# One planner, re-measured: attention with a parallel feed-forward on one core, with its sums normalised in place and zero matmuls in PE's free slots

## The chip, the core and the metric

The kernel runs on one core of a Trainium2 chip. The metric is the device time of one execution in microseconds (us). Its engines are PE (TensorE, matrix products into PSUM), ACT (ScalarE, activations), DVE (VectorE, elementwise work), POOL (GpSimd, here only setup) and SP, which issues the transfers.

## The reference

One normalised input feeds two branches, whose results are added to it. Attention has 32 query heads of width 20 and one shared key and value head, over 2048 positions.

```python
xn = _layernorm(x, axis=-1)                       # x: 1 x 2048 x 640
q = (xn @ wq).reshape(B, S, H, Dh).transpose(0, 2, 1, 3)   # H = 32, Dh = 20
k = xn @ wk                                       # one key head
v = xn @ wv
scores = jnp.einsum("bhqd,bkd->bhqk", q, k) * (Dh ** -0.5)
p = _softmax(scores, axis=-1)
o = jnp.einsum("bhqk,bkd->bhqd", p, v)
A = o.transpose(0, 2, 1, 3).reshape(B, S, H * Dh) @ wo
B_ = _silu(xn @ w1) @ w2                          # F = 1728
return x + A + B_
```

## The kernel before, in words

**Work.** The 2048 queries are cut into 4 chunks of 512. A unit is one head of one chunk; 128 units make 43 groups of 3 (the last has 2). A group walks over 16 tiles of 128 keys, one step each, 688 steps in all. A step t does the following.

- S (`do_S`, L616): up to three matmuls of 32 rows, one for each unit, write three 128x512 score banks; even and odd steps use two sets of three banks (`par3`). S of step t therefore waits until the readers of step t-2 are done.
- exp: ACT takes two or three banks in one instruction (L632) and writes them into a ring of `NBLK` slots, `E`. In a DVE step the third bank goes to DVE (L646), which computes the exponential from bits: after up to `ZB` = 4 such blocks, `flush_z` issues three instructions over all of them (L693, L696, L697). `want_dve` (L587) makes a step a DVE step when DVE's planned backlog is under `DVE_TH`.
- PV: the values times each block, four 32-column matmuls side by side (L656 for ACT's blocks, L662 and L664 for DVE's two factors), accumulated over the 16 steps in bank 6 (`UBANK`). A PV frees the slots of the ring that it read.

**End of a group** (`end_group`, L706). DVE copies bank 6 to `U` (L713). Then bank 6 is free for the next group. Four matmuls by a 0/1 matrix transpose `U` (L718) into bank 7 (`XBANK`), as a job among the others; DVE takes the reciprocal of the sums (L726) and multiplies (L743) into `o`.

**Projections.** All other matmuls are jobs that share bank 7, one after the other: queries of the next chunk (`q_job`, L755, evacuated by DVE at L767), the hidden layer (`h_job`, L781, tanh on ACT at L789 and product on DVE at L794), transposes of `o` (`oT_job`, L805) and the output (`out_job`, L828 and L834, evacuated at L841 or L848). `fill_chunk` (L872) gives each job the step from which it may start, evenly by number of jobs over `PACE` = 0.9 of the chunk's steps.

**Order.** Everything is unrolled by a planner (`Sched`) that runs before the kernel: each engine takes, at its planned time, the ready operation with the lowest priority number; durations are formulas such as `t_dve_ps`, and `LAT` is the delay until another engine sees a result. What comes out is a fixed order for each engine, with semaphore waits for each dependence on another engine. PE's order is made in `step` (L491). S comes first as soon as it is ready; otherwise PV or a job is chosen, in the mode that PE is in if possible, since another tile shape costs `SWITCH`; the choice is not made if it would end later than `limit`, which is when S is ready, or `S_LEAD` before the running exp ends, whichever is later. PV goes ahead of jobs when `PV_PRESS` = 6 steps are waiting.

**Prologue and tail.** The first 56 us load and normalise the input (statistics on DVE), transpose it and make keys and values, with the first steps among them. After the last step there remain the last output projections.

Of the kernel before, what the change touches and what calls it, by code (L numbers as in the profile page):

```python
# [15 lines left out]
P = 128  # L16
D = 640
H = 32
# [25 lines left out]
NBLK = 26  # L44
# [3 lines left out]
SWITCH = 0.10  # L48
S_LEAD = 0.62
PV_PRESS = 6  # L50
DVE_TH = 3.2
PACE = 0.9


class Op:
    __slots__ = ("eng", "dur", "fn", "deps", "prio", "seq", "end", "avail", "idx", "inc", "inc_no", "sem",
                 "on_sched", "name", "dma", "mode", "start", "mm")
# [207 lines left out]
def t_dve_ps(n):  # L265
    return n / 960.0 + 0.085
# [14 lines left out]
def t_act(n):  # L281
    return n / 1200.0 + 0.094
# [21 lines left out]
class Builder:  # L304
# [17 lines left out]
    def alloc(self):  # L322
# [36 lines left out]
        self.eps = sb([P, 1], F32)  # L359
        self.XS = 11  # L360
# [27 lines left out]
    def steps_init(self):  # L388
        self.groups = []
        u = 0  # L390
        while u < NUNITS:
            self.groups.append(list(range(u, min(u + 3, NUNITS))))
            u += 3
        self.NG = len(self.groups)
        self.T = self.NG * KT
        self.s_next = 0
        self.pv_q = deque()
        self.pv_wait = deque()
        self.misc = deque()
# [11 lines left out]
        self.pv_started = False  # L411
        self.pro_left = True
# [78 lines left out]
    def step(self, now):  # L491
# [51 lines left out]
        nxt = min(sr, pv_r, job_r)  # L543
        if choice is None:
            return nxt
        if choice == "PV":
            d = 0.216 + self.switch("PV")
        else:
            d = (job if job is not None else cand[0]).mms[0][0] + self.switch("M")
        if sr < INF and now + d > limit + 1e-9:  # L550
            return nxt if nxt > now else sr
        if choice == "PV":
            op = self.pv_q.popleft()
            op.dur = d
            if not self.pv_started:
                self.pv_started = True
                op.deps |= sc.deps_of((), [("B", UBANK)])
            self.pe_mode = "PV"
            sc.commit(op, now)
        else:  # L560
            if job is None:
                job = cand.popleft()
                job.bank = self.bank_for_job()[1]
                self.cur_job = job
            self.do_mm(job, now, d)
        return True
# [9 lines left out]
    def do_mm(self, job, now, d):  # L576
        fn = job.mms.pop(0)[1]
        b = job.bank
        op = self.sc.new("pe", d, lambda pe: fn(pe, b), job.reads, [("B", b)], name=job.name, queue=False)
        self.pe_mode = "M"  # L580
# [6 lines left out]
    def want_dve(self, t):  # L587
        if self.pro_left:
# [8 lines left out]
    def do_S(self, t, now):  # L597
# [12 lines left out]
        def fn(pe):  # L610
            ins = None
            for j, x in enumerate(us):
# [8 lines left out]
                    name=f"S{t}", queue=False)  # L621
        self.pe_mode = "S"
# [29 lines left out]
        def pfn(pe):  # L652
# [6 lines left out]
            if dv:  # L659
# [8 lines left out]
                    name=f"PV{t}", mode="PV", queue=False)  # L668
        self.pv_wait.append((pv, dv))
# [36 lines left out]
    def end_group(self, g):  # L706
        sc = self.sc
        us = self.groups[g]
        up = g % 2
# [4 lines left out]
        sc.new("dve", t_dve_ps(QW), evac, [("UB",)], [("U", up)], prio=2.0, name=f"Uev{g}")  # L714
        mms = []
        for qt in range(4):
            def f(pe, b, qt=qt):
                return pe.matmul(self.bk(b, qt * 64, qt * 64 + 64), self.U[0:rows, up, qt * P:(qt + 1) * P],  # L718
                                 self.stk[0:rows, :], start=True, stop=True)
            mms.append((0.16, f))  # L720

        def consume(b):
            xv = self.bk(b, 0, 256).rearrange("p (q z) -> p q z", q=4)[:, :, 0:63].rearrange(
                "p q (i r) -> p q i r", i=3)
            rl = self.rL[:, up, :, :]
            sc.new("dve", 0.11, lambda v: v.reciprocal(rl, xv[:, :, :, DH]), [("B", b)], [("rL", up)], prio=2.5,  # L726
                   name=f"rcp{g}")
            nh = len(us)
            for c in sorted(set(x // H for x in us)):
                js = [j for j, x in enumerate(us) if x // H == c]  # L730
                qs = [j if j < nh - 1 else 2 for j in js]
                h0 = us[js[0]] % H
                n = len(js)
                runs = [(qs, h0)]
                if qs != list(range(qs[0], qs[0] + n)):
                    runs = [([q], h0 + i) for i, q in enumerate(qs)]
                for rq, hh in runs:
                    m = len(rq)
                    dst = self.o[:, c % 2, :, hh * DH:(hh + m) * DH].rearrange("p q (i d) -> p q i d", d=DH)
                    src = xv[:, :, rq[0]:rq[0] + m, 0:DH]  # L740
                    r0 = rl[:, :, rq[0]:rq[0] + m]
                    rb = bass.AP(self.rL, r0.offset, [list(r0.ap[0]), list(r0.ap[1]), [1, m], [0, DH]])
                    sc.new("dve", t_dve_ps(4 * m * DH), lambda v, dst=dst, src=src, rb=rb: v.tensor_tensor(  # L743
                        dst, src, rb, ALU.mult), [("B", b), ("rL", up)],
                        [("o", c % 2, hh + i) for i in range(m)], prio=2.5, name=f"nrm{g}")
                self.norm_made[c] += n
        self.urgent.append(Job(f"UT{g}", mms, [("U", up), ("stk",)], consume))


    def q_job(self, c, ht, step=-1, act=False):  # L750
# [8 lines left out]
        def consume(b):  # L759
# [6 lines left out]
            else:  # L766
                sc.new("dve", t_dve_ps(QW), lambda v: v.tensor_scalar(dst, self.bk(b), C1, self.offq[:, :],  # L767
                                                                      ALU.mult, ALU.add),
                       [("B", b), ("offq",)], ks, prio=3.0, name=f"qev{c}_{ht}")
# [5 lines left out]
    def h_job(self, c, fk, step):  # L775
# [9 lines left out]
        def consume(b):  # L785
# [4 lines left out]
                   prio=3.0, name=f"th{c}_{fk}")  # L790
            ks = [("hT", fk)]
            if c == 0:
# [3 lines left out]
                [("B", b), ("tb", tp)], ks, prio=3.0, name=f"hp{c}_{fk}")  # L796
# [3 lines left out]
    def oT_job(self, c, i, step=-1):  # L800
        sc = self.sc
        mms = []
        for k in range(DC):
# [3 lines left out]
            mms.append((0.07, f))  # L807

        def consume(b):
            src = self.bk16(b)[:, 0:DC * P].rearrange("p (c t) -> p c t", c=DC)  # L810
            sc.new("dve", t_dve_ps(D), lambda v: v.tensor_copy(self.oT[:, :, i * P:(i + 1) * P], src),
                   [("B", b)], [("oT", i)], prio=3.0, name=f"oT{c}_{i}")
# [3 lines left out]
    def out_job(self, c, i, e, step=-1, ffn=True, attn=True):  # L816
# [21 lines left out]
        def consume(b):  # L838
            src = self.bk(b, 0, 320)
            if not attn:  # L840
                sc.new("dve", t_dve_ps(320), lambda v: v.scalar_tensor_tensor(  # L841
                    out=self.yx[:, i, e0:e0 + 320], in0=src, scalar=0.5, in1=self.xres[:, i, e0:e0 + 320],
                    op0=ALU.mult, op1=ALU.add), [("B", b), ("xres", i)], [("yx", i, e), ("w1",)], prio=3.0, name=f"y{n}_{e}")
# [6 lines left out]
                op0=ALU.mult, op1=ALU.add), [("B", b), rk], [("ost", sl, e)], prio=3.0, name=f"out{n}_{e}")  # L850
# [21 lines left out]
    def fill_chunk(self, c, t):  # L872
        jobs = []
        if c >= 1:
            for i in range(4):
                if c == 1:
                    self.load_xres(0, i)
                jobs.append(lambda s, i=i: self.oT_job(c - 1, i, s))
            for i in range(4):
                for e in range(2):  # L880
                    jobs.append(lambda s, i=i, e=e: self.out_job(c - 1, i, e, s))
        if c + 1 < QC:
            for ht in range(HT):
                jobs.append(lambda s, ht=ht: self.q_job(c + 1, ht, s))
        for fk in range(FC):
            jobs.append(lambda s, fk=fk: self.h_job(c, fk, s))
        if c == QC - 1:
            for i in range(4):
                for e in range(2):
                    jobs.append(lambda s, i=i, e=e: self.out_job(c, i, e, s, attn=False))  # L890
# [15 lines left out]
    def prologue(self):  # L906
# [52 lines left out]
        pool(0.2, lambda g: g.tensor_copy(self.idb[:, :], self.idf[:, :]), [("idf",)], [("idb",)])  # L959
        pool(0.1, lambda g: g.memset(self.eps[:, :], EPS), [], [("eps",)])  # L960
# [112 lines left out]
        def tr_job(n):  # L1073
            xs = n % 4
            mms = []
            for k in range(DC):
# [3 lines left out]
                mms.append((0.07, f))  # L1080

            def consume(b):
# [5 lines left out]
                else:  # L1088
                    sc.new("dve", t_dve_ps(D), lambda v: v.tensor_copy(dst, src), [("B", b)], [("xnT", n)],
# [115 lines left out]
```

## Time and profile before

| | |
|---|---|
| median of 3 runs | 910.75 us (904.34 to 915.66) |
| profiled execution | 904.07 us |
| its span, first to last instruction | 902.2 us |
| mean granted clock of PE | 0.888 |
| instructions | 15485, of them 6099 matmuls, 1281 on DVE, 755 on ACT |
| HBM | 11.36 MB read, 2.62 MB written, 15 GB/s over the span |

In the shares of busy time, each engine has its busy us, share of the span and number of instructions. PE's matmuls are pipelined and their ends are modelled, so that a matmul of 512 columns shows about 0.39 us although the next one starts 0.22 us after it. A group row has the line, the engine, the operation, what it writes and reads, its shape and count, then busy us, the mean ns of one, and the idle time of the engine just before, with what ended it. A row of the waits says who waited for whom: us in total, times, longest. In a table of windows each row has the stretch in us from the span's start, its length, busy us and count for each engine (PE, PEld for weight loads, DVE, ACT, POOL), the granted clock (1.00 is full), and the share and rate of DMA. In the timeline a row has its start, its length and what ran; "[0.35 <-DVE ...]" is the engine's idle time before it and what ended it.

### The profile page before, as it was taken

To read this page: it belongs to the slowest core of one execution; us is meant where nothing else is said; L and a number is where in the kernel's file an instruction comes from. 1 tells how busy PE (TensorE), PEld (TensorE's weight loads), DVE (VectorE), ACT (ScalarE), POOL (GpSimd) and SP (SyncE) were. 2 spreads that over 40 slices of the span, in tenths; PEclk is the share of its full clock that TensorE was granted. 3 is DMA by queue.
4 is the path that set the end of the run, shared out by engine and by line. 5 is a ranking of instruction groups with operands and counts; after the bars stand their busy time and mean duration, and the time that the engine had idled before them with its cause. 6 is when DMAs were issued, how large, how long until landed. Compare 5 with 4: busy or idle time off the path is not lost. (4 is left out here: it accounts for less than half of the span.)

```text
span 902.2 us, 15485 instructions
## 1 busy us (share of the span) xinstructions
PE 763.0 (85%) x6099; PEld 259.3 (29%) x6099; DVE 782.5 (87%) x1281; ACT 760.4 (84%) x755; POOL 26.5 (3%) x53
## 2 busy tenths in 40 slices
PE   4779887878889999888779999987789998888887
PEld 2322322222223432222213433222223342222334
DVE  7759989988888989899997999999978978878995
ACT  4469999998888799999988888999987868989980
POOL 4600000000000000000000000000000000000000
PEclk9589989887659999899967999999979898969999
DMA  9300000000000010000000000000000010000000
GB/s 305 113 1 1 1 1 2 1 1 1 1 1 16 16 30 1 1 1 1 1 1 1 30 16 16 1 1 1 1 1 1 30 31 1 1 1 1 1 1 30
DMA packets 12408, 14.97 MB, mean 17 GB/s; under 512 B 2544, under 2 KB 11696, under 8 KB 12336
## 3 DMA queue, kind: packets, MB, share of 16 engines
q1 hardware_dynamic: 11024, 13.93, 4.7%
q8 instruction: 49, 0.80, 0.4%
q10 hardware_dynamic: 1312, 0.05, 0.1%
q14 instruction: 23, 0.19, 0.1%
HBM read 11.36 MB, written 2.62 MB: 15 GB/s over the span
## 5 line engine op out<-in xcount | busy, mean ns | idle before, releaser
L632 ACT ACTIVATE sbt<-psall 128x1024 bf16<-128x1024 f32 (+2 forms) x688 | 730.6, 1143 | 104.8 <-PE psall L616 52.3
L646 DVE TENSOR_SCALAR sbt<-psall 128x512 int16<-128x512 f32 x503 | 340.7, 685 | 75.1 <-PE psall L616 72.4
L616 PE MATMUL psall<-sbt 32*128 32x512 bf16 x2048 | 293.2, 422 | 77.0 <-ACT sbt L632 57.6
L656 PE MATMUL psall<-sbt 128*32 128x512 bf16 x1545 | 226.1, 428 | 23.5 <-DVE sbt L697 12.1
L662 PE MATMUL psall<-sbt 128*32 128x512 bf16 x503 | 181.0, 426 | 0.0
L664 PE MATMUL psall<-sbt 128*32 128x512 bf16 x503 | 173.6, 428 | 0.0
L616 PEld LDWEIGHTS psall<-sbt 32*128 32x128 bf16 x2048 | 69.4, 92 | 319.3 <-ACT sbt L632 144.4
L696 DVE TENSOR_TENSOR sbt<-sbt 128x2048 bf16<-128x2048 bf16 x126 | 152.7, 1212 | 1.3
L781 PE MATMUL psall<-sbt 128*128 128x512 bf16 (+1 forms) x280 | 90.5, 422 | 7.6 <-DVE sbt L794 4.8
L656 PEld LDWEIGHTS psall<-sbt 128*32 128x32 bf16 x1545 | 55.0, 99 | 127.4 <-issue 54.1
L693 DVE TENSOR_SCALAR sbt<-sbt 128x2048 int16<-128x2048 int16 x126 | 86.7, 688 | 2.9
L828 PE MATMUL psall<-sbt 128*128 128x320 bf16 x448 | 85.1, 307 | 0.8 <-DVE sbt L841 0.4
L697 DVE TENSOR_SCALAR sbt<-sbt 128x2048 int16<-128x2048 int16 x126 | 85.5, 679 | 0.2
L828 PEld LDWEIGHTS psall<-sbt 128*128 128x128 bf16 x448 | 36.6, 98 | 43.6 <-issue 28.6
L755 PE MATMUL psall<-sbt 128*128 128x512 bf16 x160 | 45.1, 390 | 3.0 <-DVE sbt L767 1.7
L662 PEld LDWEIGHTS psall<-sbt 128*32 128x32 bf16 x503 | 41.5, 98 | 0.0
L794 DVE SCALAR_TENSOR_TENSOR sbt<-sbt,psall 128x512 bf16<-128x512 bf16 (+1 forms) x56 | 38.0, 678 | 2.5 <-ACT sbt L789 2.4
L718 PE MATMUL psall<-sbt 128*128 128x64 f32 x172 | 35.9, 311 | 4.5 <-DVE sbt L794 2.3
L789 ACT ACTIVATE sbt<-psall 128x512 bf16<-128x512 f32 (+1 forms) x56 | 34.3, 612 | 6.3 <-PE psall L781 4.5
L664 PEld LDWEIGHTS psall<-sbt 128*32 128x32 bf16 x503 | 37.4, 97 | 0.0
L781 PEld LDWEIGHTS psall<-sbt 128*128 128x128 bf16 (+1 forms) x280 | 21.1, 102 | 51.4 <-issue 26.7
L718 PEld LDWEIGHTS psall<-sbt 128*128 128x128 f32 x172 | 27.9, 214 | 25.0 <-issue 11.2
(67 smaller groups left out, 293.5 us busy)
## 6 DMA issues: line engine op xcount, KB each, us to landing
sbt<-in_A_x_dram SPq DMA_DIRECT2D x32, 160.0 KB, 2.9
out_dram<-sbt SPq DMA_DIRECT2D x16, 160.0 KB, 1.8
sbt<-in_B_w_dram SPq DMA_DIRECT2D x5, 432.0 KB, 6.7
sbt<-in_B_w_dram SPq DMA_DIRECT2D x13, 160.0 KB, 5.3
sbt<-in_A_wq_dram SPq DMA_DIRECT2D x5, 160.0 KB, 3.4
sbt<-in_A_wo_dram SPq DMA_DIRECT2D x5, 160.0 KB, 6.5
sbt<-in_B_w_dram SPq DMA_DIRECT2D x1, 80.0 KB, 5.7
sbt<-in_A_wk_dram ACTq DMA_DIRECT2D x1, 25.0 KB, 2.8
```

The source lines that it names most:

```text
L616: ins = pe.matmul(self.bk(par3 + j), self.kT[r:r + SLOT, kk, kt * P:(kt + 1) * P], self.qT[r:r + SLOT, h // 4, (x // H) % 2, :], start=Tru ...
L632: return a.activation(self.E[:, b0 * QW:(b0 + na) * QW], self.ps[:, par3 * BANK:(par3 + na) * BANK], AF.Exp, scale=ACT_SCALE)
L646: return v.tensor_scalar(self.Z[:, zs, zp * QW:(zp + 1) * QW], self.bk(bb), 0.0, ZMAX, ALU.max, ALU.min)
L656: ins = pe.matmul(self.bk(UBANK, 0, QW, q * SLOT, (q + 1) * SLOT), self.v[:, kt, :], self.E[:, (b0 + j) * QW:(b0 + j + 1) * QW], start=fir ...
L662: pe.matmul(self.bk(UBANK, 0, QW, 64, 96), self.v[:, kt, :], y, start=first, stop=last, tile_position=(0, 64))
L664: ins = pe.matmul(self.bk(UBANK, 0, QW, 96, 128), self.v[:, kt, :], z, start=(gd == 0), stop=(self.last_dve_kt[g] == kt), tile_position=(0 ...
L693: sc.new("dve", t_dve_4x(w), lambda v: v.tensor_scalar(Y, Z, 0x7F, 0x3F80, ALU.bitwise_and, ALU.bitwise_or), zk, yk, prio=4.0, name="u")
L696: sc.new("dve", t_dve_2x(w), lambda v: v.tensor_tensor(yb, zb, yb, ALU.mult), zk + yk, yk, prio=4.0, name="T1")
L697: sc.new("dve", t_dve_4x(w), lambda v: v.tensor_scalar(Z, Z, 0x7F80, None, ALU.bitwise_and), zk, zk, prio=4.0, name="B")
L718: return pe.matmul(self.bk(b, qt * 64, qt * 64 + 64), self.U[0:rows, up, qt * P:(qt + 1) * P], self.stk[0:rows, :], start=True, stop=True)
L781: return pe.matmul(self.bk(b, 0, QW, 0, rows), self.w1[:, k, fk * P:fk * P + rows], self.xnT[:, k, c * QW:(c + 1) * QW], start=(k == 0), s ...
L828: return pe.matmul(self.bk(b, 0, 320), self.hT[0:rows, fk, i * P:(i + 1) * P], self.w2[0:rows, fk, e0:e0 + 320], start=(m == 0), stop=(m = ...
```

## The change

All of it is in the planner and in how the order is made; the computation is the same.

1. The planner's durations and delays get other values (`LAT`, `t_dve_ps`, `t_act`, single entries), and its limits too (`S_LEAD`, `DVE_TH`, `SWITCH`). A last step of a group is never a DVE step (`NOD`).
2. U is transposed into bank 6 itself, as one operation of four matmuls in PV's own queue. The reciprocal and the product read bank 6, so the next group's PV waits for them. These operations and all evacuations get priorities under 1.0, ahead of DVE's first exponential step.
3. The ring has 34 slots instead of 26, and PV goes first when more than 25 of them are in use.
4. `fill`: where PE has nothing to do until S or the next work is planned, and its planned busy share over the last 3.4 us is under 0.72, it gets a matmul by a zeroed tile of up to 512 columns. While a group's sum is open, it adds zeros to bank 6; otherwise it writes bank 7 when that is free.
5. A job's starting step is spread by its cost instead of by number.

```diff
-NBLK = 26
+NBLK = 34
-SWITCH = 0.10
-S_LEAD = 0.62
-PV_PRESS = 6
-DVE_TH = 3.2
-PACE = 0.9
+SWITCH = 0.105
+S_LEAD = 0.56
+PV_PRESS = 9
+DVE_TH = 4.0
+U_PRIO = 0.9
+X_PRIO = 0.95
+PACE = (0.9, 0.9, 0.9, 0.9)
+WIN = 3.4
+FILL_BELOW = 0.72
+OVER = 0.1
+NOD = 1
-LAT = {"pe": 0.20, "act": 0.09, "dve": 0.06, "pool": 0.10, "sp": 0.0}
+LAT = {"pe": 0.215, "act": 0.175, "dve": 0.14, "pool": 0.15, "sp": 0.0}
 def t_dve_ps(n):
-    return n / 960.0 + 0.085
+    return n / 960.0 + 0.067
 def t_act(n):
-    return n / 1200.0 + 0.094
+    return n / 1200.0 + 0.051
...
-        press = len(self.pv_q) + len(self.pv_wait) >= PV_PRESS
+        used = sum(o.na for o in self.pv_q) + sum(o.na for o, _ in self.pv_wait)
+        press = used > NBLK - PV_PRESS
         choice = None
-        if pv_n and self.pe_mode == "PV":
+        if pv_n and (self.pe_mode == "PV" or press or self.pv_q[0].mode == "M"):
             choice = "PV"
-        elif has_misc and self.pe_mode == "M" and not (press and pv_n >= 2):
+        elif has_misc and self.pe_mode == "M":
             choice = "M"
...
         if choice is None:
-            return nxt
+            return self.fill(now, min(nxt, limit)) or nxt
...
-        if sr < INF and now + d > limit + 1e-9:
-            return nxt if nxt > now else sr
+        if sr < INF and now + d > limit + OVER:
+            return self.fill(now, limit) or (nxt if nxt > now else sr)
...
+    def fill(self, now, until):
+        if self.s_next >= self.T and not self.pv_q:
+            return None
+        sc = self.sc
+        mode = "PV" if self.u_open else "M"
+        room = min(until, now + 0.33) - now - self.switch(mode)
+        if room < 0.08 or self.busy_share(now) > FILL_BELOW:
+            return None
+        n = min(512, int(room * 2400) // 32 * 32)
+        if self.u_open:
+            ukey = None
+
+            def fn(pe):
+                return pe.matmul(self.bk(UBANK, 0, n, 0, 32), self.zero[:, 0:32], self.zero[:, 0:n], start=False,
+                                 stop=False, tile_position=(0, 0), skip_group_check=True)
+        else:
+            r, b = self.bank_for_job()
+            if self.cur_job is not None or r > now + 1e-9:
+                return None
+            ukey = ("B", b)
+
+            def fn(pe):
+                return pe.matmul(self.bk(b, 0, n), self.zero[:, 0:P], self.zero[:, 0:n], start=True, stop=True)
...
     def want_dve(self, t):
-        if self.pro_left:
+        if self.pro_left or t % KT >= KT - NOD:
             return False
...
-        sc.new("dve", t_dve_ps(QW), evac, [("UB",)], [("U", up)], prio=2.0, name=f"Uev{g}")
-        mms = []
-        for qt in range(4):
-            def f(pe, b, qt=qt):
-                return pe.matmul(self.bk(b, qt * 64, qt * 64 + 64), self.U[0:rows, up, qt * P:(qt + 1) * P],
-                                 self.stk[0:rows, :], start=True, stop=True)
-            mms.append((0.16, f))
+        sc.new("dve", t_dve_ps(QW), evac, [("UB",)], [("U", up)], prio=U_PRIO, name=f"Uev{g}")
+
+        def ut(pe):
+            ins = None
+            for qt in range(4):
+                ins = pe.matmul(self.bk(UBANK, qt * 64, qt * 64 + 64), self.U[0:rows, up, qt * P:(qt + 1) * P],
+                                self.stk[0:rows, :], start=True, stop=True)
+            return ins
+        op = sc.new("pe", 0.5, ut, [("U", up), ("stk",)], [("UB",)], name=f"UT{g}", mode="M", queue=False)
+        self.pv_wait.append((op, False))
...
-        span = PACE * (s1 - s0)
-        for k, mk in enumerate(jobs):
-            j = mk(s0 + int(span * k / len(jobs)))
-            self.misc.append(j)
+        span = PACE[c] * (s1 - s0)
+        tot = sum(w for w, _ in jobs)
+        at = 0.0
+        for w, mk in jobs:
+            self.misc.append(mk(s0 + int(span * at / tot)))
+            at += w
```

The weights w are 1.4 for a transpose of `o`, 3.6 for an output job (2.9 without attention), 2.2 for a query job and 3.0 for a hidden-layer job.

More of the change, by code (lines that the diff above doesn't have):

```diff
@@ L359, in alloc @@
         self.eps = sb([P, 1], F32)
+        self.zero = sb([P, 512], BF16)
         self.XS = 11
@@ L554, in step @@
             op.dur = d
+            op.work = 0.216
+            self.u_open = op.kt < KT - 1
+            self.pe_mode = op.mode
             if not self.pv_started:
@@ L565, in step, with busy_share @@
             self.do_mm(job, now, d)
+        return True
+    def busy_share(self, now):
+        a = now - WIN
+        tot = 0.0
+        for op in reversed(self.sc.order["pe"]):
+            if op.end <= a:
+                break
+            tot += op.end - max(a, op.end - op.work)
+        return tot / WIN
+    def fill(self, now, until):
[19 more added lines that the diff above has]
+                return pe.matmul(self.bk(b, 0, n), self.zero[:, 0:P], self.zero[:, 0:n], start=True, stop=True)
+        z = sc.lastw.get(("zero",))
+        if z is None or z.avail is None or z.avail > now:
+            return None
+        op = sc.new("pe", n / 2400.0 + self.switch(mode), fn, [("zero",)], [ukey] if ukey else [],
+                    name="fill", queue=False)
+        op.work = n / 2400.0
+        self.nfill += 1
+        self.pe_mode = mode
+        sc.commit(op, now)
         return True
@@ L621, in do_S @@
                     name=f"S{t}", queue=False)
+        op.mm = nh
+        op.work = 0.216
         self.pe_mode = "S"
@@ L668, in do_S @@
                     name=f"PV{t}", mode="PV", queue=False)
+        pv.mm = na + (2 if dv else 0)
+        pv.kt = kt
+        pv.na = na
         self.pv_wait.append((pv, dv))
```

100 lines of the change are left out of this document (54 added, 46 removed).

## Prediction

> **What bounds the kernel now.** I read the shares of busy time first, then the table of waits, then the granted clock by stretches, then the timeline around two places.
>
> ```profile
> span 902.2 us, 15485 instructions
> PE 763.0 (85%) x6099; PEld 259.3 (29%) x6099; DVE 782.5 (87%) x1281; ACT 760.4 (84%) x755; POOL 26.5 (3%) x53
> ...
> PEclk9589989887659999899967999999979898969999
> ```
>
> No engine is full: DVE 87%, ACT 84%. The two share the exponentials, so both are the bound together, and what is to be had is their common idle time. The profiled execution took 904.07 us, 1.9 us more than its span. The waits (engine, line, who is waited for: us in total, times, longest) say where ACT and DVE stand idle:
>
> ```profile
> DVE sbt L646 <- PE psall L616: 72.4, 120, 1.9
> ...
> ACT sbt L632 <- PE psall L616: 52.3, 72, 6.1
> ACT sbt L632 <- PE psall L664: 30.1, 25, 3.3
> ...
> ACT sbt L632 <- PE psall L656: 18.7, 13, 3.3
> ```
>
> The first two are waits for scores (S). The last two, 48.8 us in 38 waits of 1.3 us on average, are waits for PV matmuls that still read the slots of the exp ring: the ring is full. The third thing is PE's clock. Rows of equal windows (us of the window; busy us and count of PE, PEld, DVE, ACT, POOL; granted clock; DMA):
>
> ```profile
> 196.32:199.74 3.42, 3.09 (x29) 0.76 (x21) 3.07 (x6) 3.42 (x5) 0.00 (x0) 1.00 0.00 0
> 199.74:203.15 3.41, 1.08 (x13) 0.33 (x10) 3.41 (x6) 3.41 (x5) 0.00 (x0) 1.00 0.00 0
> 203.15:206.56 3.41, 3.16 (x20) 1.43 (x19) 3.38 (x7) 2.78 (x3) 0.00 (x0) 0.50 0.00 0
> 206.56:209.98 3.42, 3.42 (x25) 0.61 (x22) 1.77 (x3) 2.37 (x2) 0.00 (x0) 0.50 0.00 0
> ```
>
> In the second row ACT and DVE are completely busy and PE, ahead of them, has nothing to do: 1.08 us of 3.41. In the next row its clock is 0.50, and ACT falls to 2.78 and 2.37 us, for now PE is the slow one. So PE loses its clock just when the other two run best. Over all 23 stretches at clock 0.50 between 56.4 and 880 us, and over the 24 stretches at 1.00 between them, two tables of windows sum to
>
> ```profile
> sum 170.68, PE 157.97 PEld 39.79 DVE 137.77 ACT 131.21 POOL 0.00; mean PE 6.87 PEld 1.73 DVE 5.99 ACT 5.70 POOL 0.00
> ```
> ```profile
> sum 652.92, PE 555.32 PEld 191.83 DVE 598.20 ACT 601.38 POOL 0.48; mean PE 23.14 PEld 7.99 DVE 24.92 ACT 25.06 POOL 0.02
> ```
>
> ACT is busy 76.9% of the time at half clock and 92.1% at full clock. Single stretches at full clock show what remains:
>
> ```profile
> 404.54:455.74 51.20, 40.02 (x350) 12.15 (x349) 49.38 (x75) 50.91 (x54) 0.00 (x0) 1.00 0.01 1
> ...
> 687.84:715.15 27.31, 25.55 (x223) 10.21 (x220) 25.46 (x39) 21.09 (x21) 0.00 (x0) 1.00 0.04 14
> 721.98:745.87 23.89, 22.93 (x203) 9.52 (x200) 17.83 (x30) 16.57 (x17) 0.00 (x0) 1.00 0.10 29
> ```
>
> The first is nearly perfect (ACT 99%). In the other two, where the output projection of a chunk runs, PE is nearly full and ACT waits for it.
>
> **The change, part by part.**
>
> *Zero matmuls, clock.* If the half-clock stretches ran like the others, their 131.21 us of ACT work would take 131.21/0.921 = 142.5 us instead of 170.68: 28 us. The fills go in when the modelled busy share of PE over 3.4 us is under 0.72, and the window that lost the clock had 1.08/3.41 = 0.32, the one before it kept it with 0.90 by this (pipelined) count. They need a PE that is idle by plan, which the second row above is; they don't help where PE is blocked by an unplanned wait. I take 25 of the 28. The bounds are 0 (zero data don't count as work) and 28.
>
> The Trainium skill, "TensorE: Matmul & The Clock Gate", section "HAM oscillation — how this bites in real kernels", states that the clock is lost through PE-idle gaps of more than about 3.4 us. By that rule this kernel would keep its clock without fills and this term would be nothing; the trace disagrees, for the clock fell after a window in which PE worked 1.08 us.
>
> The prologue has half clock too:
>
> ```profile
> 22.30:42.60 20.30, 13.58 (x115) 7.60 (x115) 16.62 (x64) 8.15 (x7) 13.01 (x17) 0.50 0.34 117
> 42.70:49.40 6.70, 5.13 (x64) 2.52 (x59) 1.51 (x4) 5.18 (x4) 2.65 (x5) 1.00 0.15 42
> 49.60:56.30 6.70, 5.56 (x50) 2.84 (x47) 1.51 (x4) 2.79 (x2) 0.48 (x1) 0.50 0.00 0
> ```
>
> In the first row DVE (16.62 of 20.30) is the longest and would hide a faster PE; in the last PE is, and half of 5.56 is 2.8. With something from the first: 4 us, bounds 0 and 10 (half of 13.58 + 5.56).
>
> What fills cost: PE changes the shape of its tiles for them. The timeline shows the price of a change of shape:
>
> ```profile
> 196.04 0.38 PE L656 MATMUL psall<-sbt 128*32 128x512 bf16 x2
> ...
> 196.26 0.38 PE L656 MATMUL psall<-sbt 128*32 128x512 bf16 x2
> ...
> 198.60 0.39 PE L616 MATMUL psall<-sbt 32*128 32x512 bf16 x3
> ...
> 198.92 0.60 PE L781 MATMUL psall<-sbt 128*128 128x512 bf16 x2
> ```
>
> Same shape: 0.22 us from start to start. From S to another shape 0.32: a change costs 0.10. PE's array needs, by estimate, about 0.22 us each for 688 S, 688 PV (up to four side by side) and 440 full matmuls, and about 100 us for the smaller ones: some 500 us, 0.60 of the 824. Lifting that to 0.72 of about 775 us is 58 us of zeros; at 0.15 to 0.2 us each 300 to 400 fills. 400 x 0.10 = 40 us of PE time, of which only what delays an S counts. S is planned first and a fill ends by the time S is due, so I take 4; bounds 0 and 40. The skill speaks against the fills here too: "TensorEngine Tiling (Array Packing)", section "Key Properties", states that changing the tiling mode drains TensorE. The 0.32 against 0.22 agrees; with every drain on the path the sum would be 36 us worse.
>
> S may now be started 0.56 us before the running exp ends instead of 0.62. What S needs:
>
> ```profile
> 863.90 0.39 PE L616 MATMUL psall<-sbt 32*128 32x512 bf16 x3
> ...
> 864.34 0.69 DVE L646 TENSOR_SCALAR sbt<-psall 128x512 int16<-128x512 f32 x1 [0.56 <-PE psall L616]
> ```
>
> 0.44 us from S to its reader, 0.54 with a change of shape: just enough, cost nothing; 688 x 0.02 = 14 us if it is short by that much.
>
> *Deeper ring.* 8 more slots. Groups by line and shape (count | busy us, mean ns | idle before, by what ended it):
>
> ```profile
> L632 ACT ACTIVATE sbt<-psall 128x1024 bf16<-128x1024 f32 x499 | 491.9, 1039 | 63.3 <-PE psall L616 29.8 <-PE psall L664 19.8 <-PE psall L656 10.9
> L646 DVE TENSOR_SCALAR sbt<-psall 128x512 int16<-128x512 f32 x503 | 340.7, 685 | 75.1 <-PE psall L616 72.4
> ...
> L632 ACT ACTIVATE sbt<-psall 128x1536 bf16<-128x1536 f32 x179 | 259.9, 1462 | 41.5 <-PE psall L616 22.4 <-PE psall L664 10.3 <-PE psall L656 7.8
> L656 PE MATMUL psall<-sbt 128*32 128x512 bf16 x1545 | 226.1, 428 | 23.5 <-DVE sbt L697 12.1 <-DVE sbt L713 8.5 <-ACT sbt L632 2.1
> ...
> L713 DVE CAST sbt<-psall 128x512 fp32r<-128x512 f32 x43 | 29.4, 684 | 4.4 <-PE psall L664 3.5 <-PE psall L656 0.7
> ```
>
> There are 688 steps (43 groups of 16). A step uses 1545/688 = 2.25 slots and lasts 1.2 us (824 us from 56.4 to 880, less the 15 or so steps before them): 8 slots are 3.6 steps, 4.3 us, more than the longest ring wait of 3.3 us. So alone it could remove all 48.8 us. But it isn't alone: PV is now pressed only with more than 25 of 34 slots in use (before with 6 steps waiting, about 13.5 of 26), and the next part holds PV back.
>
> *U normalised in its own bank.* The timeline at the end of a group:
>
> ```profile
> 418.66 0.68 DVE L713 CAST sbt<-psall 128x512 fp32r<-128x512 f32 x1
> ...
> 419.40 0.40 PE L656 MATMUL psall<-sbt 128*32 128x512 bf16 x3 [0.35 <-DVE sbt L713]
> ...
> 420.26 0.63 PE L718 MATMUL psall<-sbt 128*128 128x64 f32 x4
> ...
> 421.05 0.22 DVE L726 RECIPROCAL sbt<-psall 128x12 f32<-128x12 f32 x1
> ...
> 421.74 0.40 DVE L743 TENSOR_TENSOR sbt<-psall,sbt 128x240 bf16<-128x240 f32 x1
> ```
>
> Now PV resumes 0.74 us after L713 starts, and the transposes go elsewhere later. After the change PV waits for all of it: 0.74 to the first transpose, 0.79 to the reciprocal, about 0.28 to the product, 0.40 for it and 0.1 to PE: 2.3 us, 1.6 more. Over 43 groups PV stands still 69 us longer. Nothing else on PE waits behind it by plan (S and projections go on) and the cover is the ring: 4.3 - 1.6 = 2.7 us more slack than now, against waits of 1.3 on average and 3.3 at most. If that cover is gone, late PV means full slots, then ACT, then S. I take 60% of the 48.8 as gained, 29 us (bounds 0 and 49), and 5 us lost at group ends (bounds 0 and 69). The bank for projections is freed of 43 uses of 1.9 us (420.26 to 422.14); since the projections are paced by step numbers, I count nothing.
>
> *Model, priorities, spread.* Durations and delays in the planner change only the order of instructions. Exponentials on DVE are barred in a group's last step, which moves up to 43 x 503/688 = 31 blocks to ACT; the higher backlog limit (4.0 for 3.2) and cheaper entries move some to DVE. By the rows of L632 a block more costs ACT 1462 - 1039 = 423 ns: 31 x 0.42 = 13 us on ACT if nothing comes back. I count 0, between -5 and 13. Projections spread by their cost: the output jobs get 29% of a chunk's steps (28.8 of 99.6 by the new weights) where 8 of 34 jobs had 24%. The two crowded stretches lost 51.2 - 37.66/0.921 = 10 us; I take 5, bounds 0 and 10. Evacuations now go ahead of DVE's share of the exponentials; each holds it up 0.7 us at most and frees its bank as much sooner: nothing.
>
> *Sum*, against the profiled 904: -25 -4 +4 -29 +5 -5 = -54, so 850. The median of the three runs is 910.75, 6.7 above the profiled one; runs differ by how much clock they lose, I suppose, so most of this should go with the losses. I add 2: **852**.
>
> **Rivals.**
>
> *The floor is reached* (0.14): the stretch 404.54:455.74 is the rule. ACT's 131.21 + 601.38 = 732.6 us at 98% take 748 instead of 823.6: 904 - 76 - 4 = 824. For it: waits for PE are all the idle time there is. Against it: DVE's chains (three instructions on up to four blocks) still come in lumps.
>
> *The ring waits only move* (0.20): late pressing and the U bank eat the 8 slots, so the 29 us stay: 879, as a median 881.
>
> *The zeros don't hold the clock* (0.10), because zero data don't count or the losses come with blocked PE: 25 + 4 us stay, 879 to 883; the change wouldn't do what it says. The rows speak against it: the planned idle time was in a window with both other engines full.
>
> *U's bank on the path* (0.06), the slower side: if DVE takes rcp and product behind a long instruction and the ring is full by then, the 69 us are ACT idle time: 904 - 29 + 69 = 944 with the ring gain gone. It decides from about 1.3 us a group on, where the gains are used up. Against it: PE's 15% idle time lets PV catch up.
>
> **How the numbers follow.** The forecast has 0.50, by itself 835 to 870. About 2% (18 us) can be told from no change here. Below 892: forecast, floor and most of the two rivals at 880: 0.84. Within 2%: 0.09, their upper tails. Slower: 0.07, the U bank and what I haven't seen. The range for 8 in 10 leaves out half of the floor case, the slower side and a little of the tails: 815 to 893.
>
> **What would show it.** Right: mean clock 0.96 or more with few half-clock stretches after 60 us; some 300 to 400 new matmuls; ACT's waits for PV lines down from 49 us to about 20; L713 to next PV about 2.3 us and yet no ACT gap at group ends; ACT and DVE both at 90%. Wrong: clock still near 0.89; PV waits as long as now but behind the product of L743; ACT waiting for S behind fills; DVE down and ACT up by tens of us.

## The result, and the profile after

The changed kernel takes 821.68 us (median of 4 runs, 818.49 to 825.41) against 913.0 us before (the three runs above and a fourth): 0.9016 of the time, 95% interval 0.894 to 0.909. This lies inside the forecast range of 815 to 893 us, but 30 us under its likeliest case of 852 us; it is the time of the rival "the floor is reached" (824 us). One execution of run 10 below was more than 1.5% slower than the fastest of its kernel and is left out of the median given there. The page after:

```profile
span 816.7 us, 15973 instructions
PE 755.5 (93%) x6358; PEld 262.4 (32%) x6358; DVE 759.3 (93%) x1267; ACT 750.1 (92%) x755; POOL 26.8 (3%) x54
...
PEclk9999998999999999999989999999999999999999
```

ACT and DVE have nearly the same work as before (750 and 759 us busy, before 760 and 783), packed into 86 us less. The mean granted clock is 0.985 instead of 0.888. Two tables of windows after the first 56.4 us, the four stretches at half clock and the five at full clock up to the last exp, sum to

```profile
sum 20.50, PE 19.49 PEld 3.81 DVE 15.22 ACT 14.89 POOL 0.00; mean PE 4.87 PEld 0.95 DVE 3.81 ACT 3.72 POOL 0.00
```
```profile
sum 712.70, PE 669.17 PEld 224.52 DVE 693.21 ACT 701.22 POOL 0.00; mean PE 133.83 PEld 44.90 DVE 138.64 ACT 140.24 POOL 0.00
```

Before, 170.68 us ran at half clock, now 20.5. At full clock ACT is busy 98.4% (before 92.1%) and DVE 97.3%: what one good stretch showed before is now the rule. The waits:

```profile
ACT sbt L693 <- PE psall L675: 32.7, 45, 7.3
...
DVE sbt L707 <- PE psall L675: 17.6, 43, 1.6
...
PEld psall L717 <- DVE sbt L812: 7.9, 25, 0.9
```

L693 is the exp, L675 the scores and L717 the PV matmuls (lines have moved). No row of ACT waiting for PV is left, where there were 48.8 us; DVE's waits for scores fell from 72.4 to 17.6 us. The third row is the new wait of PV for the product behind U. The fills are the groups

```profile
L605 PE MATMUL psall<-sbt 128*32 128x512 bf16 (+9 forms) x179 | 50.4, 368 | 0.0
...
L614 PE MATMUL psall<-sbt 128*128 128x512 bf16 (+6 forms) x88 | 25.6, 413 | 3.5 <-POOL sbt L1030 1.5 <-DVE sbt L862 1.2 <-DVE sbt L1160 0.8
```

179 on open sums and 88 in bank 7: only 267. At the end of one group, with the longest such pause of all, the timeline now reads (rows of ACT, DVE's U path, PV, and one of DVE's exponential steps, L761):

```profile
390.64 4.39 ACT L693 ACTIVATE sbt<-psall 128x1536 bf16<-128x1536 f32 x4
...
391.13 0.68 DVE L778 CAST sbt<-psall 128x512 fp32r<-128x512 f32 x1
...
392.66 0.63 PE L784 MATMUL psall<-sbt 128*128 128x64 f32 x4
...
393.46 0.22 DVE L796 RECIPROCAL sbt<-psall 128x12 f32<-128x12 f32 x1
...
394.15 0.39 DVE L812 TENSOR_TENSOR sbt<-psall,sbt 128x240 bf16<-128x240 f32 x1
...
394.70 0.82 ACT L857 ACTIVATE sbt<-psall 128x512 bf16<-128x512 f32 x1
...
395.18 4.44 ACT L693 ACTIVATE sbt<-psall 128x1024 bf16<-128x1024 f32 x4
...
396.85 0.68 DVE L761 TENSOR_SCALAR sbt<-sbt 128x2048 int16<-128x2048 int16 x1
...
398.31 0.39 PE L717 MATMUL psall<-sbt 128*32 128x512 bf16 x2
```

PV stands still from 391 to 398 us, and ACT runs through it with only a tanh (L857) between its exps: the ring covers it. The product is done at 394.54 us; the rest of the pause belongs to DVE's exponentials, since the first PV is that of a DVE step, whose last factor (L761) is ready at 397.53 us. Over the 42 group ends that a PV follows, the time from the start of U's copy to the next PV is 3.70 us on average after, 1.91 before: 1.8 us more (predicted: 1.6).

### The profile page after: what moved, and what is told of

It is laid out like the page before. It is cut to its first block, busy times and chain, and to the rows that moved or that the text cites. A ratio compares the mean times of both kernels' runs of the same rounds, so it can differ in the third digit from the quotient of the medians.

```text
span 816.7 us, 15973 instructions
## 1 busy us (share of the span) xinstructions
PE 755.5 (93%) x6358; PEld 262.4 (32%) x6358; DVE 759.3 (93%) x1267; ACT 750.1 (92%) x755; POOL 26.8 (3%) x54
## 4 chain that ended last, share of the span: by engine, by line
PE 36%; DVE 32%; ACT 24%; issue 7%; POOL 1%; POOLq 0%; ACTq 0%
ACT sbt L693 22%; PE psall L675 11%; DVE sbt L707 11%; PE psall L717 9%; PE psall L896 6%; DVE sbt L760 6%; DVE sbt L757 4%; ACT sbt L857 2%; PE psall L902 2%; PE psall L849 2%; DVE sbt L761 2%; PE psall L823 2%; DVE sbt L778 2%; DVE sbt L862 1%; PE psall L605 1%
## 5 line engine op out<-in xcount | busy, mean ns | idle before, releaser
L693 ACT ACTIVATE sbt<-psall 128x1024 bf16<-128x1024 f32 (+1 forms) x688 | 726.6, 1185 | 34.5 <-PE psall L675 32.7
L707 DVE TENSOR_SCALAR sbt<-psall 128x512 int16<-128x512 f32 x495 | 330.6, 681 | 19.3 <-PE psall L675 17.6
L675 PE MATMUL psall<-sbt 32*128 32x512 bf16 x2048 | 269.7, 388 | 38.6 <-ACT sbt L693 22.6
L717 PE MATMUL psall<-sbt 128*32 128x512 bf16 x1553 | 205.7, 389 | 2.8 <-DVE sbt L761 1.4
L723 PE MATMUL psall<-sbt 128*32 128x512 bf16 x495 | 160.5, 389 | 0.0
L675 PEld LDWEIGHTS psall<-sbt 32*128 32x128 bf16 x2048 | 70.0, 91 | 268.6 <-ACT sbt L693 86.4
L725 PE MATMUL psall<-sbt 128*32 128x512 bf16 x495 | 154.0, 389 | 0.0
L849 PE MATMUL psall<-sbt 128*128 128x512 bf16 (+1 forms) x280 | 85.6, 392 | 2.3 <-DVE sbt L862 1.6
L896 PE MATMUL psall<-sbt 128*128 128x320 bf16 x448 | 84.9, 302 | 1.2 <-DVE sbt L916 0.7
L761 DVE TENSOR_SCALAR sbt<-sbt 128x2048 int16<-128x2048 int16 x124 | 84.5, 682 | 0.4
L717 PEld LDWEIGHTS psall<-sbt 128*32 128x32 bf16 x1553 | 51.4, 95 | 91.5 <-issue 47.6
L605 PE MATMUL psall<-sbt 128*32 128x512 bf16 (+9 forms) x179 | 50.4, 368 | 0.0
L857 ACT ACTIVATE sbt<-psall 128x512 bf16<-128x512 f32 (+1 forms) x56 | 38.0, 678 | 0.0
L723 PEld LDWEIGHTS psall<-sbt 128*32 128x32 bf16 x495 | 37.1, 95 | 0.0
L902 PE MATMUL psall<-sbt 128*128 128x320 bf16 x160 | 32.2, 303 | 2.7 <-DVE sbt L879 2.7
L725 PEld LDWEIGHTS psall<-sbt 128*32 128x32 bf16 x495 | 34.0, 94 | 0.0
L778 DVE CAST sbt<-psall 128x512 fp32r<-128x512 f32 x43 | 29.5, 685 | 4.8 <-PE psall L717 4.5
```

The lines of the kernel that those rows point to most:

```text
L675: ins = pe.matmul(self.bk(par3 + j), self.kT[r:r + SLOT, kk, kt * P:(kt + 1) * P], self.qT[r:r + SLOT, h // 4, (x // H) % 2, :], start=Tru ...
L693: return a.activation(self.E[:, b0 * QW:(b0 + na) * QW], self.ps[:, par3 * BANK:(par3 + na) * BANK], AF.Exp, scale=ACT_SCALE)
L707: return v.tensor_scalar(self.Z[:, zs, zp * QW:(zp + 1) * QW], self.bk(bb), 0.0, ZMAX, ALU.max, ALU.min)
L717: ins = pe.matmul(self.bk(UBANK, 0, QW, q * SLOT, (q + 1) * SLOT), self.v[:, kt, :], self.E[:, (b0 + j) * QW:(b0 + j + 1) * QW], start=fir ...
L723: pe.matmul(self.bk(UBANK, 0, QW, 64, 96), self.v[:, kt, :], y, start=first, stop=last, tile_position=(0, 64))
L725: ins = pe.matmul(self.bk(UBANK, 0, QW, 96, 128), self.v[:, kt, :], z, start=(gd == 0), stop=(self.last_dve_kt[g] == kt), tile_position=(0 ...
```

## The experiments

**Theory 1**: the gain is a sum of separate terms, above all the held clock and the deeper ring, as the prediction had it. **Theory 2**: the gain is the better order that a truer model makes, and clock and waits only follow from it. The ratios are against the kernel before, whose medians were 909.03, 913.45 and 911.92 us beside runs 1 to 4, 5 to 8 and 9 to 12. The changed kernel's 0.9016 was measured apart from them.

**1. Fills planned, not issued.**

```diff
-                return pe.matmul(self.bk(UBANK, 0, n, 0, 32), self.zero[:, 0:32], self.zero[:, 0:n], start=False,
-                                 stop=False, tile_position=(0, 0), skip_group_check=True)
+                return None
...
-                return pe.matmul(self.bk(b, 0, n), self.zero[:, 0:P], self.zero[:, 0:n], start=True, stop=True)
+                return None
```

> The changed kernel with its order unchanged, but the zero matmuls are left out of PE's list (their planned time stays empty), so only what they do on the chip is taken away. Theory 1 (a sum of separate parts, with the clock as one): the clock falls back to about 0.89 to 0.92 and the time rises by the prediction's terms for it, 28 + 4, to about 850 us. Theory 2 (the gain is the order that a truer planner model makes; the clock follows from it, as PE is starved less): clock above 0.95 and less than 10 us lost, under 832 us.

850.14 us, ratio 0.9328 (0.9266 to 0.9390), clock 0.909. Every other instruction is the same, in the same order on each engine. So 267 matmuls of zeros, which compute nothing, are worth 28 us. The waits and the clock without them:

```profile
PEclk9569999897757999999887999999997999999999
```
```profile
ACT sbt L692 <- PE psall L674: 57.6, 69, 7.7
```

The clock falls again and again as before the change, and ACT waits 25 us longer for scores (57.6 against 32.7). Theory 1.

**2. The ring at 26 slots.**

```diff
-NBLK = 34
+NBLK = 26
```

> The changed kernel with 26 slots in the exp ring again (pressing then starts above 17). Theory 1: ACT waits for PV lines again, some 30 to 49 us, and the time is 850 to 870 us. Theory 2: the planner knows the ring's size and presses PV in time, under 10 us of such waits and under 832 us.

846.24 us, 0.9294 (0.9254 to 0.9334): 25 us lost, just under the first expectation's range and far from the second's. ACT waits for PV again, though less than before the change:

```profile
ACT sbt L693 <- PE psall L725: 15.5, 19, 3.2
...
ACT sbt L693 <- PE psall L717: 5.0, 7, 1.2
```

**3. U in bank 7.** The transposes are a job in bank 7 again, and reciprocal and product read it there.

```diff
-        op = sc.new("pe", 0.5, ut, [("U", up), ("stk",)], [("UB",)], name=f"UT{g}", mode="M", queue=False)
...
-        self.pv_wait.append((op, False))
...
+        self.urgent.append(Job(f"UT{g}", mms, [("U", up), ("stk",)], consume))
```

> The changed kernel with U transposed into bank 7 as an urgent job again, as before the change (new priorities and durations kept). Theory 1 (the prediction's term): PV resumes about 1.6 us earlier at each of 43 group ends, nothing else moves, 0 to 5 us gained, 816 to 822 us. Rival: the 43 uses of bank 7 now stand in the way of the projections and of fills, 5 to 20 us lost, 827 to 842 us.

832.54 us, 0.9155 (0.9115 to 0.9195): 11 us lost. Both theories were half right. PV resumes earlier (1.54 us after the copy instead of 3.70), and the last exp starts at 780.6 us, 9 us before that of the changed kernel (789.6). But the tail after it takes 49 us instead of 27, because projections were left over. Groups from 781 us to the end:

```profile
L893 PE MATMUL psall<-sbt 128*128 128x320 bf16 x112 | 17.0, 300 | 1.5 <-DVE sbt L859 1.5
L846 PE MATMUL psall<-sbt 128*128 128x512 bf16 (+1 forms) x58 | 13.3, 380 | 0.2 <-issue 0.2
```

Those are 12 hidden-layer jobs and all 8 output jobs of the last chunk. The changed kernel has from 790 us on

```profile
L896 PE MATMUL psall<-sbt 128*128 128x320 bf16 (+1 forms) x56 | 8.9, 301 | 0.5 <-DVE sbt L909 0.5
```

only half of the output jobs and no hidden-layer job.

**4. The old model in the changed kernel** (delays, two formulas and single durations; all else as changed).

```diff
-LAT = {"pe": 0.215, "act": 0.175, "dve": 0.14, "pool": 0.15, "sp": 0.0}
+LAT = {"pe": 0.20, "act": 0.09, "dve": 0.06, "pool": 0.10, "sp": 0.0}
...
-    return n / 960.0 + 0.067
+    return n / 960.0 + 0.085
...
-    return n / 1200.0 + 0.051
+    return n / 1200.0 + 0.094
```

> The changed kernel with the planner's old durations and delays (delays, the three formulas and the single entries; limits, ring, fills and U as changed). Theory 1: order alone is worth little, 0 to 10 us lost, 822 to 832 us. Theory 2: most of the gain beyond the predicted one goes, 30 us or more lost, 850 us or more, with ACT and DVE both waiting for S longer.

825.37 us, 0.9060 (0.9021 to 0.9099). The interval overlaps the changed kernel's: nothing that can be told apart. Theory 2 falls: the model that gives the change its first words is worth a few us at most.

**5. The fills alone on the kernel before** (the function `fill`, the count of PE's busy time that it needs and the zeroed tile; nothing else is edited, but the planner lays out its order around the fills, so that the order of ACT and DVE changes too).

```diff
         if choice is None:
-            return nxt
+            return self.fill(now, min(nxt, limit)) or nxt
...
-            return nxt if nxt > now else sr
+            return self.fill(now, limit) or (nxt if nxt > now else sr)
```

> The kernel before with the zero matmuls alone (same rule and threshold, old planner values, ring, U path and limits). If the clock is a term of its own that is worth the same anywhere: clock 0.96 or more and 25 to 32 us gained, 877 to 884 us. Rival: the fills only hold the clock where the rest of the plan is right; on the old order the clock stays under 0.94 and under 12 us are gained, 897 us or more.

857.77 us, 0.9398 (0.9340 to 0.9456), clock 0.982: 56 us gained, twice the expected. The waits tell why:

```profile
ACT sbt L685 <- PE psall L668: 29.2, 38, 6.2
ACT sbt L685 <- PE psall L717: 24.9, 21, 2.1
...
ACT sbt L685 <- PE psall L709: 8.9, 6, 2.6
```

The second and third are ring waits: 33.8 us, where the kernel before had 48.8. Of these, 42.0 of the 48.8 us and 32.0 of the 33.8 us ended at full clock after the prologue. So 10 of the 15 us that went lay in stretches that show a full clock. That they were the aftermath of a lost clock fits, but is not shown by itself, as the order changed too.

**6. The ring alone on the kernel before.**

```diff
-NBLK = 26
+NBLK = 34
```

> The kernel before with 34 slots in the exp ring alone. If the ring is a term of its own: the waits of ACT for PV lines (48.8 us) nearly go, and what 26 slots cost in the changed kernel (25 us) or more is gained, 870 to 884 us. Rival: without a held clock the PE starves and slows as before and the ring's waits turn into waits for S: under 10 us gained, 899 us or more.

871.04 us, 0.9537 (0.9468 to 0.9607): 42 us gained, although the clock stays at 0.902. The rival falls: ACT's waits for scores rise only from 52.3 to 62.1 us while its waits for PV nearly go.

```profile
ACT sbt L632 <- PE psall L616: 62.1, 80, 6.5
...
ACT sbt L632 <- PE psall L664: 3.4, 2, 1.9
```

**7. Old limits and priorities in the changed kernel.**

```diff
-S_LEAD = 0.56
-DVE_TH = 4.0
-OVER = 0.1
-NOD = 1
+S_LEAD = 0.62
+DVE_TH = 3.2
+OVER = 1e-9
+NOD = 0
...
-        sc.new("dve", t_dve_ps(QW), evac, [("UB",)], [("U", up)], prio=U_PRIO, name=f"Uev{g}")
+        sc.new("dve", t_dve_ps(QW), evac, [("UB",)], [("U", up)], prio=2.0, name=f"Uev{g}")
```

> The changed kernel with the old limits and priorities: U and evacuations behind DVE's first exponential step (2.0, 2.5, 3.0), a group's last step may be a DVE step, backlog limit 3.2, S by 0.62 us before the exp's end and nothing over it. The four parts undone so far sum to 68 of the 88 us. If the rest lies in these limits: 10 to 25 us lost, 832 to 847 us. Rival, the prediction's term (nothing): within 5 us of 822.

834.28 us, 0.9128 (0.9063 to 0.9194): 10 to 13 us lost, at the edge of what can be told apart. The page's groups show a balance that tips:

```profile
L693 ACT ACTIVATE sbt<-psall 128x1024 bf16<-128x1024 f32 (+1 forms) x688 | 740.6, 1270 | 31.9 <-PE psall L675 27.7 <-PE psall L717 2.4 <-PE psall L725 1.1
L707 DVE TENSOR_SCALAR sbt<-psall 128x512 int16<-128x512 f32 x459 | 309.7, 684 | 49.5 <-PE psall L675 46.6
```

The other evacuations, the reciprocal and the product get their old priorities (2.5 and 3.0) as well. With the cheaper entries of the new model, a backlog limit of 3.2 and DVE steps allowed to the end of a group, DVE gets only 459 blocks (495 in the changed kernel) and idles 46.6 us for scores, while ACT is the longer one. Which of the limits does it was not tried one by one.

**8. Projections spread by number.**

```diff
-        for w, mk in jobs:
-            self.misc.append(mk(s0 + int(span * at / tot)))
-            at += w
+        for k, (w, mk) in enumerate(jobs):
+            self.misc.append(mk(s0 + int(span * k / len(jobs))))
```

> The changed kernel with the projections spread evenly by their number again. The prediction's term: 5 us lost (0 to 10), 822 to 832 us, with ACT idle again where the output jobs crowd. Rival: with PE's clock held the crowding costs nothing, or the new spread costs something at the chunk's end: 817 to 822 us.

818.53 us, 0.8977 (0.8912 to 0.9042): no difference from the changed kernel that can be told, as the rival had it.

**9. Fills and ring together on the kernel before** (runs 5 and 6 in one).

> The kernel before with the zero matmuls and 34 slots together. Alone they gained 56 and 42 us. If they are independent: 98 us, about 815 us, all of the change. If part of the ring's waits came from the lost clock (ACT's waits for PV fell from 48.8 to 33.8 us with the fills alone), the sum is smaller: 70 to 85 us, 828 to 843 us, and U's bank and the limits make up the rest.

839.03 us, 0.9225 (0.9165 to 0.9286): 73 us, less than 56 + 42 and within the range expected if the two share part of their gain. By the ratios the other 19 us of the change are in U's bank, limits, model and spread.

**10. U in bank 7 and 26 slots** (runs 2 and 3 in one).

> The changed kernel with U in bank 7 and 26 slots, the fourth corner of that square (821.7 as changed, 846.2 with 26 slots, 832.5 with U in bank 7). If the ring is the cover of U's own bank (the prediction's step), U's bank costs more at 26 slots: this is faster than 846, 825 to 840 us. Rival, the two are independent: 821.7 + 24.6 + 10.9, 852 to 862 us.

850.11 us (median of three), 0.9320 (0.9252 to 0.9389), not told apart from run 2's 0.9294. The expected 825 to 840 us did not come; the time is just under the rival's range. With 34 slots U's own bank gains 11 us, with 26 some 2 to 4: the sign of the prediction's cover is there, but too small to be shown by these intervals. The traces show more: the last exp starts at 790.5 us here and at 811.7 us in run 2, 21 us apart where it was 9 us with 34 slots, and the tails are 50.6 and 32.7 us. So by these traces U's own bank delays the exps more when the ring is short, and relief at the tail pays for it. Up to 7 of the 21 us may be this execution, which was the fastest of its kernel (842.84 us). No cost of U's own bank can be told even at 26 slots.

**11. U in bank 7, projections started earlier.**

```diff
-PACE = (0.9, 0.9, 0.9, 0.9)
+PACE = (0.8, 0.8, 0.8, 0.8)
```

> The changed kernel with U in bank 7 and the projections started earlier (their steps spread over 0.8 instead of 0.9 of a chunk in all four chunks). With U in bank 7 the last exp started at 780.6 us, 9 us before that of the changed kernel, but projections were left for a tail of 49 us. If the tail was only late starting: the tail shrinks to 30 us or less and the time is 805 to 816 us, better than the change. If bank 7 itself is full: the tail stays above 40 us, 825 us or more.

835.14 us, 0.9175 (0.9130 to 0.9219), with a tail of 49.4 us and again all 8 output jobs in it. The projections were not waiting for their starting step; they could not be done sooner. This fits a full bank 7, but PE's free slots, which the jobs also need, were not separated from it, so this cause stays open. By an estimate from the traces (from a job's first matmul to its last reader, between 60 us and the last exp) bank 7 is held 86% of the time in run 3, 103 us of it for U, and 88% in the changed kernel.

**12. The last chunk's projections started earlier in the changed kernel.**

```diff
-PACE = (0.9, 0.9, 0.9, 0.9)
+PACE = (0.9, 0.9, 0.9, 0.8)
```

> The changed kernel with the projections of the last chunk alone started earlier (0.8 instead of 0.9). Its tail after the last exp is 27 us, with 56 of the output's feed-forward matmuls in it (8.9 us). If they wait for their starting step: 3 to 8 us gained, 813 to 819 us. If bank 7 or the evacuations hold them: within 2 us of 821.7, or slower for crowding the last chunk.

820.45 us, 0.9014 (0.8974 to 0.9053): the same time, the same 27 us tail with the same 56 matmuls. No kernel tried here is faster than the changed one by more than the intervals.

## Why the prediction was right or wrong

*Direction and what bounds* were right: ACT and DVE share one bound, PE's late scores and the full ring were their idle time, and both went for the most part. The likeliest case was too cautious: 850 us for the profiled execution, which took 818.49. Nearly all its errors lie on one side, too little gain, so the range held because it had room for the floor and not because errors cancelled.

*Clock: 25 us of 28, and 4 in the prologue.* Mis-sized. The step that failed is "if the half-clock stretches ran like the others". It charged the lost clock only with the time inside those stretches. Alone, the fills gained 56 us (run 5). The windows of run 5 at half and at full clock, from 56.4 us to its last exp, sum to

```profile
sum 30.72, PE 28.51 PEld 8.09 DVE 24.47 ACT 22.83 POOL 0.00; mean PE 5.70 PEld 1.62 DVE 4.89 ACT 4.57 POOL 0.00
```
```profile
sum 746.20, PE 689.51 PEld 237.57 DVE 700.35 ACT 701.79 POOL 0.00; mean PE 114.92 PEld 39.59 DVE 116.72 ACT 116.97 POOL 0.00
```

In the profiles 902.2 us became 855.9. These 46 us can be estimated in parts, at the 92.1% of the prediction. The half-clock term gave 22 us: 30.72 - 22.83/0.921 = 6 of its 28 stay. At full clock ACT is busier as well, 94.0% for 92.1%, and its 701.79 us of work would have taken 762 us instead of 746: 16 us. The prologue gave 4, and some 5 are less ACT work. The remaining 10 us between 46 and 56 are the runs: the profiled execution before was its fastest. The prediction supposed that this spread would go with the lost clock, and added only 2 us for it.

The same windows of the other kernels show what each part does:

| kernel | us at half clock | ACT busy at full clock |
|---|---|---|
| before | 170.7 | 92.1% |
| fills alone (run 5) | 30.7 | 94.0% |
| ring alone (run 6) | 141.2 | 97.0% |
| fills and ring (run 9) | 17.1 | 97.9% |
| changed, fills not issued (run 1) | 124.9 | 98.0% |
| changed | 20.5 | 98.4% |

In the prologue ACT got more done in the same 56.4 us (this row of the windows after, that of before and that of run 1 below it):

```profile
0.00:56.40 56.40, 45.92 (x388) 21.60 (x388) 38.31 (x132) 32.97 (x31) 26.79 (x54) 0.97 0.50 168
```
```profile
0.00:56.40 56.40, 33.82 (x289) 18.26 (x289) 35.28 (x123) 27.02 (x25) 26.01 (x52) 0.76 0.51 167
```
```profile
0.00:56.40 56.40, 34.55 (x295) 18.36 (x295) 34.44 (x125) 27.02 (x25) 26.83 (x54) 0.75 0.51 167
```

5.95 us of ACT's work, predicted 4; run 1 shows that they are the zeros' doing.

*Zeros count as work*: right, by run 1. Their cost of shape changes (4 of up to 40 us) could not be seen by itself; the number of fills (300 to 400) was 267.

*Ring: 29 of 48.8.* 42 us alone (run 6), 25 us as the last part put in (run 2), 16 to 19 us on top of the fills (runs 5 and 9). 29 lies inside these, but it was added to the clock's term as if the two shared nothing, while run 9 shows 25 us shared (73 against 98). Most of it can be the 16 us above: both parts make ACT busier at full clock, and they can do so only once. The sum of the two terms, 54, stayed under 73 all the same, since the clock's term was too small.

*U's own bank: 5 us lost.* Wrong in sign: 11 us gained (run 3). The mechanism as told was right (1.8 us later PV per group, 9 us in the last exp's start; run 10's trace fits the ring as its cover). Its levels came from a single group end, 0.74 us before and 2.3 after, where the averages are 1.91 and 3.70. But "the bank for projections is freed of 43 uses of 1.9 us; ... I count nothing" was the step that failed. That relief is 22 us at the tail (49 against 27), since the projections do not only follow step numbers: they fall behind. Whether for want of the bank or of PE's time is open (run 11).

*Limits and priorities: nothing, between 5 us gained and 13 lost.* By run 7 they gain 10 to 13 us, beyond the good end of that range, though at the edge of what can be told. The feared loss, 31 blocks moved from DVE to ACT, did not come: DVE has 495 blocks for 503. *Spread: 5 us gained.* Nothing that can be told (run 8). From 687 to 746 us, where the crowded stretches lay, ACT waits 13.7 us for PV and 2.8 us for scores before the change: the ring was most of that loss. *Model: order only.* Right (run 4).

*Fills' cost: 4 us lost*, see the zeros above; no run separates it. *The rivals.* "The ring waits only move" and "the zeros don't hold the clock" fell to runs 2, 6 and 1. "U's bank on the path" did not come about at 34 slots, and no cost of it can be told at 26. "The floor is reached" was the case: its 98% for ACT is measured as 98.4% at full clock. Its evidence, one stretch with ACT at 99% at full clock, deserved more than 0.14: apart from its waits for scores and for PV, no row of ACT's waits before the change had more than 4.5 us.

## What to carry to other kernels

A lost clock can cost more than the slowdown inside the half-clock stretches: 46 us of the profile against 22 here, with a short ring. So look also at the waits in the full-clock stretches that follow, where the engines behind PE are still short of work or of buffers. Take one part out of the finished kernel and put the same part alone into the old one: the two numbers (28 and 56 us, 25 and 42 us) show how far parts overlap, which a list of single gains hides. A bank, buffer or queue that many jobs share in turn is worth costing by its own busy time: here its relief came out at the tail and not where it was made.

## What the runs showed of the hardware

PE's clock follows the share of time in which the array has work, not what it computes. Matmuls of zeros held it, 179 of 267 of them 32 columns wide and so on a quarter of the array: 0.985 with them, 0.909 without, with all other instructions the same.

The granted clock changes only at steps of 3.41 us in these traces. The array's working share in each such step can be estimated from the matmuls' starts and column counts, with 0.216 us for 512 columns from start to start at full clock and twice that at half clock (0.40 to 0.43 us measured). Between 56.4 us and the last exp before the change, the clock fell after 23 steps with a share of 0.19 to 0.43 and stayed full after 167 with 0.43 to 0.91. It came back after 23 with 0.80 to 0.93 and stayed at half after 27 with 0.41 to 0.79. Over all 14 traces it fell 109 times, always after a share of 0.45 or less, and stayed full 2768 times, in all but 19 of them after 0.44 or more. It came back after no share under 0.67. So in this kernel it takes less work to keep the clock than to get it back. The kernel's own limit for fills, 0.72 of PE's planned time, lies well above 0.45; a lower one was not tried.

The Trainium skill, "TensorE: Matmul & The Clock Gate", section "HAM oscillation — how this bites in real kernels", has the rule that no PE-idle gap may be longer than about 3.4 us. These traces do not agree that this is enough: between the prologue and the last exp PE's longest pause (from one matmul's start to the next, less 0.216 us) was 1.7 us in run 1 and 1.8 us before the change, and the clock was lost 18 and 23 times.
